# Strided half of x for two batches transposed by the DMA queue through the idle raw tile of k, with new lists for the order of the work

## The chip, the cores and the metric

The kernel runs on one core of one Trainium2 chip. The time is the device time of one execution, in microseconds (us). Before the change it is 287.94 us (median of three runs, 287.9 to 288.31). Other numbers come from one profiled execution of the same kernel, which took 288.18 us.

## The reference

Two layers in a row, on 8 batches of 576 tokens. Inputs are float32, and so is the output.

```python
# attention: q, k, v are (8, 8, 576, 64)
scores = q @ k^T / 8
mask_local   = (rel >= 0) & (rel < 32)                      # heads 0 to 3
mask_strided = (rel >= 0) & (pos_k % 32 == pos_q % 32)      # heads 4 to 7
attn = softmax(where(mask, scores, -1e9)) @ v
# mlp: x is (4608, 512), w_in (512, 2048), w_out (2048, 512)
x = attn.transpose(0, 2, 1, 3).reshape(4608, 512)
h = x @ w_in
out = (h * tanh(softplus(h))) @ w_out
```

## The kernel before, in words

The 4608 tokens of the second layer are worked in nine blocks of 512 (`t` = 0 to 8); the attention works in eight batches of 576 (`b` = 0 to 7). While block `t` goes through the second layer, batch `t + 1` goes through the attention, so that block `t + 1` finds its x. The x of the last four batches lies transposed in one ring, `xT`: 128 partitions by four chunks of columns. Chunks 0 and 1 hold the local heads, chunks 2 and 3 the strided ones.

**The second layer.** Each of its two matrix products is written as seven products of half size instead of eight (sums of weights and of x are made on VectorE). A block's first product goes in four groups `g`. In a list, `5:2` is product 5 of group 2, four matmuls of 256 columns; `1c`, `5c` are copies out of PSUM, `6c` and `7c` additions on VectorE that product 7 and product 4 wait for; `E`, `H`, `Z` are the activations on ScalarE; `x:0` to `x:3` are the sums of x. The second product of block `t - 1` runs in block `t`: `m5:0` is half of product 5, eight matmuls; `m1c`, `m5c`, `m6c`, `m7c`, `m3c`, `m4c` empty its banks, `g:1` to `g:3` and `n` are sums of the activations (`gs`), `st` stores the result.

**The attention.** `ld` loads a raw tile by GpSimd's queue (`ks`, `qs`: the strided heads; `kl`, `ql`: the local ones; `vs`, `vl`: the values). Batches 0 to 2 are transposed by TensorE (`T`, with the copy `t`), later ones by DMA transposes that SyncE (SP) issues (`D`). `q:s0` makes scores, `e` the exponentials, `k` multiplies by the mask, `v` is the product with the values, and `r` divides by the sums into `x_s` (72 partitions, strided) or `x_l` (96, local). `sp` and `sh` spread and share the values. From batch 2 on, `x_l` goes into `xT` by two DMA transposes of SP (`y:0`, `y:1`), and `x_s` by TensorE: `X:0:a` is eight transposes (line 322) into the spare PSUM bank `at`, and `xc:0:a:D` the copy from there into `xT` (line 112 on VectorE). `hold` is a small copy on GpSimd that waits for the DMA transposes of x, so that the loads queued behind it are issued after them.

**Order.** Nothing is reordered by a scheduler: the lists (`IN`, `SECOND`, `THIRD`, `MAIN`, `PLAIN`, `LAST`) are played word by word, and each engine works off its own instructions in that order, waiting on semaphores where an operand or a buffer isn't free. `IN` is the start and block 0, `SECOND` block 1, `THIRD` block 2, `MAIN` blocks 3 to 6 (batches 4 to 7), `PLAIN` blocks 7 and 8, which have no attention beside them, and `LAST` the second product of block 8. The loads of batch `b` are issued in blocks `b - 2` and `b - 3`; after batch 7 there are none left.

## Time and profile before

| | |
|---|---|
| median of the runs | 287.94 us |
| profiled execution | 288.18 us |
| its span, first to last instruction | 286.4 us |
| TensorE busy (matmuls) | 277.1 us, 97% |
| VectorE busy | 222.3 us, 78% |
| ScalarE busy | 193.8 us, 68% |
| GpSimd busy | 53.6 us, 19% |
| granted TensorE clock | 1.000 |

Blocks start, by TensorE's timeline, at about 59 us (block 1), 77 (block 2), 106.1, 134.7, 163.2 and 191.8 (blocks 3 to 6), 220.3 and 245.4 (blocks 7 and 8); block 8's second product begins at 270.

How to read it: a matmul's duration in the rows is from its issue to its modelled end, and matmuls overlap in the array, so what one costs in a dense stretch is the step from its start to the start of the next. In a row of the timeline stand the start, the duration of the group, engine, line, operation, tiles (written <- read), forms and the count; in brackets the idle time before it and what ended that. "SPq" and "POOLq" rows are issues of DMAs. Tiles `set`, `ee` and `at` are PSUM banks.

### The profile page before, as it was taken

The numbers are of one execution on the slowest core, as the hardware profiler recorded it, in microseconds if no ns is written. First come the engines' busy times: TensorE is split into PE (matmuls) and PEld (weight loads), VectorE is DVE, ScalarE is ACT, GpSimd is POOL, SyncE is SP. The second block draws the span as 40 slices with busy tenths as digits, with TensorE's granted clock in tenths as the row PEclk, the third lists the DMA queues.
The fourth block names the chain that finished last, engine by engine and source line by source line (L and its number), as shares of the span: only waits on it lengthen the run. The fifth ranks groups of instructions, "written<-read, shape, count | busy, mean of one in ns | idle before, by whom it ended". The sixth has DMA issues, their size and how long they took to land.

```text
span 286.4 us, 7693 instructions
## 1 busy us (share of the span) xinstructions
PE 277.1 (97%) x3274; PEld 227.8 (80%) x3274; DVE 222.3 (78%) x378; ACT 193.8 (68%) x293; POOL 53.6 (19%) x66
## 2 busy tenths in 40 slices
PE   8789999989999999999999999999999999999994
PEld 3556845658988898988899889988898888888884
DVE  1388869799998897989698969896989666756652
ACT  3686883499769777669776977697769127506920
POOL 8424241250007001700350054001000000000000
PEclk9999999999999999999999999999999999999999
DMA  6999999999959989999899979997050021003003
GB/s 102 176 206 201 205 183 199 110 219 163 150 95 92 127 145 113 233 153 155 228 141 131 179 199 165 127 176 203 11 190 2 2 94 54 0 3 146 2 0 146
DMA packets 101394, 37.45 MB, mean 131 GB/s; under 512 B 83040, under 2 KB 96992, under 8 KB 101360
## 3 DMA queue, kind: packets, MB, share of 16 engines
q0 software_dynamic: 61824, 18.85, 65.3%
q1 hardware_dynamic: 39248, 17.86, 26.7%
q8 instruction: 25, 0.41, 0.6%
q10 hardware_dynamic: 288, 0.25, 0.3%
q14 instruction: 9, 0.07, 0.1%
HBM read 37.87 MB, written 9.44 MB: 165 GB/s over the span
## 4 chain that ended last, share of the span: by engine, by line
PE 91%; DMA 3%; DVE 2%; ACT 1%; issue 1%; POOL 1%; DVEq 0%; ACTq 0%; POOLq 0%
PE set L121 57%; PE ee L121 21%; PE at L291 5%; PE at L121 4%; DMA vraw<-in_v_dram 3%; PE at L322 1%; PE ee L192 1%; PE ee L322 1%; DVE ee L115 0%; DVE qTl L112 0%; PE set L291 0%; PE ee L186 0%; ACT gT L649 0%; DVE x_l L305 0%; POOL ks L126 0%
## 5 line engine op out<-in xcount | busy, mean ns | idle before, releaser
L121 PEld LDWEIGHTS <-wis 128*128 128x128 bf16 x578 | 55.9, 98 | 11.4 <-issue 2.6
L121 PEld LDWEIGHTS <-gs 128*128 128x128 bf16 x512 | 48.8, 98 | 6.0
L121 PEld LDWEIGHTS <-gT 128*128 128x128 bf16 x448 | 42.1, 98 | 9.5
L121 PEld LDWEIGHTS <-w_in 128*128 128x128 bf16 x436 | 40.9, 97 | 8.6 <-issue 1.3
L121 PE MATMUL set<-w_out,gT 128*128 128x256 bf16 (+1 forms) x304 | 46.8, 295 | 0.0
L121 PE MATMUL set<-xT,w_in 128*128 128x256 bf16 (+1 forms) x296 | 45.7, 278 | 0.5 <-ACT set L110 0.3
L121 PE MATMUL set<-xs,wis 128*128 128x256 bf16 x280 | 42.0, 272 | 0.2 <-DVE ee L115 0.2
L420 ACT ACTIVATE gT<-set 128x1024 bf16<-128x1024 f32 x35 | 35.9, 1025 | 8.0 <-PE set L121 7.9
L110 ACT COPY set<-set 128x512 f32<-128x512 f32 x36 | 20.7, 574 | 18.4 <-PE set L121 17.9
L115 DVE TENSOR_TENSOR hh<-set,hh 128x512 f32<-128x512 f32 x35 | 24.0, 686 | 7.2 <-PE set L121 6.2
L115 DVE TENSOR_TENSOR ee<-set,hh 128x512 f32<-128x512 f32 x35 | 24.4, 697 | 5.7 <-PE set L121 5.3
L121 PE MATMUL set<-wos,gs 128*128 128x256 bf16 x224 | 28.5, 273 | 0.0
L416 ACT ACTIVATE gT<-ee 128x512 bf16<-128x512 f32 x35 | 20.2, 597 | 3.4 <-PE ee L121 3.2
L418 ACT ACTIVATE gT<-hh 128x512 bf16<-128x512 f32 x35 | 21.6, 632 | 0.9 <-DVE hh L115 0.6
L638 POOL COPY hold<-xT 1x2 bf16<-1x2 bf16 x6 | 3.3, 556 | 100.5 <-DMA xT<-x_l 98.5
L115 DVE TENSOR_TENSOR gs<-gT,gs 128x2048 bf16<-128x2048 bf16 x16 | 19.5, 1217 | 2.0 <-PE at L121 1.8
L121 PE MATMUL ee<-xs,wis 128*128 128x256 bf16 x140 | 21.0, 273 | 0.0
L121 PE MATMUL set<-xs,w_in 128*128 128x256 bf16 x140 | 21.0, 272 | 0.0
L121 PE MATMUL ee<-xT,wis 128*128 128x256 bf16 x140 | 21.0, 273 | 0.0
L115 DVE TENSOR_TENSOR gs<-gT 128x2048 bf16<-128x2048 bf16 x16 | 19.4, 1215 | 0.0
L305 DVE TENSOR_TENSOR x_s<-at,rden 72x768 bf16<-72x768 f32 (+1 forms) x22 | 18.8, 856 | 0.8
L266 DVE TENSOR_TENSOR Pl<-Pl,consts_sb 128x768 bf16<-128x768 bf16 x21 | 11.6, 554 | 8.6 <-ACT Pl L258 6.4
(127 smaller groups left out, 450.9 us busy)
## 6 DMA issues: line engine op xcount, KB each, us to landing
...
ks<-in_k_dram POOLq DMA_DIRECT2D x8, 288.0 KB, 10.6
qs<-in_q_dram POOLq DMA_DIRECT2D x8, 288.0 KB, 10.0
vraw<-in_v_dram POOLq DMA_DIRECT2D x8, 288.0 KB, 8.9
ql<-in_q_dram POOLq DMA_DIRECT2D x8, 288.0 KB, 10.3
vl<-in_v_dram POOLq DMA_DIRECT2D x8, 288.0 KB, 12.0
...
```

The costliest lines, as they stand in the source:

```text
L110: Sc.copy(out_, in_)
L115: eng.tensor_tensor(out=out_, in0=a, in1=b, op=op)
L121: PE.matmul(o, lhsT=lhsT, rhs=rhs, start=start, stop=stop, skip_group_check=True)
L192: PE.transpose(tr[64 * e:64 * e + 64, PL * j:PL * j + PL], src[0:PL, 2 * hp + e, j, :], ident[0:PL, 0:PL],)
L266: meng.tensor_tensor(out=pm, in0=pm, in1=mk[0:n, :].unsqueeze(1).unsqueeze(1).to_broadcast([n, 2, nu, w]), op=ALU.mult,)
L291: PE.matmul(po[:, (n - n0) // per, (n - n0) % per, :], lhsT=pt[0:r, c0:c0 + 128], rhs=rhs, start=True, stop=True,)
L305: Dv.tensor_tensor(out=xo, in0=po[0:m, :, :, 0:D], in1=rd.unsqueeze(3).to_broadcast([m, nb, per, D]), op=ALU.mult,)
L322: PE.transpose(tr[:, n * j:n * j + n], x[0:n, u:u + 2, :].rearrange("p u d -> p (u d)"), ident[0:n, 0:n],)
L416: Sc.activation(o[:, 0:2, 256:512], two(E), AF.Mish)
L418: Sc.activation(o[:, 2:4, 256:512], two(h[:, 1, :]), AF.Mish)
L420: Sc.activation(o[:, :, 0:256].rearrange("p (b u) n -> p b u n", b=2), SET[z][:, 0:2, :].rearrange("p b (u n) -> p b u n", u=2), AF.Mish,)
L638: Po.tensor_copy(hold[0:1, 0:2], src)
```

## The change

In blocks 5 and 6 the strided x of batches 6 and 7 no longer goes through TensorE. `V` is one DMA transpose issued by SP: it reads `x_s` (80 rows, of which the last eight are zeros now written once at the start) and writes sixteen transposed pieces into `ks`, the raw tile of k, which no load needs again at that point. `vc:0` and `vc:1` then copy them, with a stride, into chunks 2 and 3 of `xT`. `V` stands at the end of block 5 and of block 6; the copies stand early in the following block, both on VectorE in block 6, one on ScalarE and one on VectorE in block 7. Blocks 5, 6 and 7 get lists of their own (`M5`, `M6`, `P7`), and all other lists are written anew with the same words in another order, and with some copies on another engine. In the diff most of the lists' rows are left out.

```diff
@@ -312,6 +312,19 @@
             nc.sync.dma_start_transpose(
                 xT[:, c, t0:t0 + S].rearrange("p (u n) -> p u n", u=NW),
                 x_l[0:WQ, 12 * c:12 * c + 12, :].rearrange("p u d -> p (u d)"),
+            )
+
+        def xs_dma(self):
+            nc.sync.dma_start_transpose(
+                flat(ks)[:, 0:16 * SU].rearrange("c (u n) -> c u n", u=16),
+                x_s[0:SU].rearrange("p u d -> p (u d)"),
+            )
+
+        def xs_copy(self, hf, eng):
+            t0 = (self.b % RING) * S
+            cast(
+                eng, xT[:, 2 + hf, t0:t0 + S].rearrange("p (n j) -> p n j", j=CS),
+                flat(ks)[:, 8 * SU * hf:8 * SU * hf + 8 * SU].rearrange("p (j n) -> p n j", j=CS)[:, 0:PN, :],
             )
 
         def xt(self, kind, hf, bank):
@@ -529,6 +542,7 @@
         Sc.dma_start(consts[:], consts_h.ap())
         for x in (ks, qs):
             nc.sync.dma_start(x[PN:SU].rearrange("p h x -> p (h x)"), zeros_h.ap())
+        nc.sync.dma_start(x_s[PN:SU].rearrange("p u d -> p (u d)"), zeros_h.ap())
         Dv.memset(wis[:, 0:2, 0, 0, :], 0.0)
 
         at = {}
@@ -629,6 +643,10 @@
                 at[b].xt_copy("sl"[f == "yc"], int(x[0]), BANK[x[1]], eng)
             elif f == "y":
                 at[b].xt_dma(int(x[0]))
+            elif f == "V":
+                at[b].xs_dma()
+            elif f == "vc":
+                at[b].xs_copy(int(x[0]), eng)
             elif f == "D":
                 for n in x:
                     transpose_by_dma(n)
@@ -682,80 +700,106 @@
...
         IN = (
-            "ae un:1:a un:1:a un:1:a ld:ks@0 un:1:a un:1:a un:1:a un:1:a un:1:a ld:qs@0 clear:0 ld:kl@0 b:s1:C@0 "
...
+            "ld:ks@0 ld:qs@0 un:1:a un:1:a un:1:a un:1:a un:1:a un:1:a un:1:a un:1:a clear:1 clear:0 b:s1:C@0 "
+            "un:1:a un:1:a un:1:a un:1:a T:ks0:e@0 un:1:a T:ks1:f@0 ld:kl@0 t:ks0:e:A@0 b:s0:B@0 ae t:ks1:f:D@0 "
+            "T:qs0:e@0 T:qs1:f@0 t:qs0:e:D@0 un:1:a b:s2:A@0 un:1:e ld:vs@0 sp:D un:1:e t:qs1:f:A@0 q:s2:A:b@0 "
+            "un:1:e e:s2:A@0 q:s1:C:b@0 q:s0:B:b@0 e:s1:C@0 e:s0:B@0 ld:ql@0 T:kl1:f@0 t:kl1:f:A@0 un:1:e "
...
         SECOND = (
-            "so:1:D so:2:D T:ql1:f x:0 q:s0:A so:3:D t:ql1:f:D x:1 sh:D e:s0:A T:ql0:e q:s1:H ld:ks@3 t:ql0:e:D "
-            "1:0 e:s1:H 1c:0:D q:s2:A e:s2:A k:s2:D q:l0:H x:3 5:0 q:l1:A e:l0:H q:l2:H sp:D 2:0 5c:0:A k:s0:D "
-            "6:0 x:2 e:l2:H 1:1 e:l1:A 1c:1:A 5:1 6c:0 7:0 k:l1:D 5c:1:A 2:1 6:1 ld:vl@3 v:s0:A k:s1:D 3:0 7c:0 "
...
+            "x:0 T:ql1:f so:1:D so:2:D so:3:D t:ql1:f:D x:1 q:s0:A e:s0:A T:ql0:e t:ql0:e:D q:s1:H 1:0 q:s2:A "
+            "e:s1:H sp:D sh:D q:l0:H 1c:0:D e:s2:A 5:0 e:l0:H q:l1:A q:l2:H x:2 k:s1:D x:3 5c:0:A 2:0 e:l2:H 6:0 "
+            "ld:ks@3 k:s2:D 6c:0 k:s0:D e:l1:A 1:1 5:1 7:0 7c:0 1c:1:A 2:1 5c:1:A 6:1 6c:1 v:s0:A r:s0:A 3:0 4:0 "
...
         MAIN = (
+            "m1c:A g:1 ae g:2 m5:0 m2:0 x:0 q:l0:A e:l0:A q:l1:F m2:1 m6:0 e:l1:F q:s0:F e:s0:F sh:D q:l2:A "
+            "k:l0:D m6:1 e:l2:A m6c:D k:l1:D x:1 m5:1 x:2 q:s2:F q:s1:A e:s2:F e:s1:A m7:0 m7:1 m5c:A D:ks@{n1} "
...
+        M5 = (
+            "x:0 m5:0 ld:kl@{n2} m1c:A m5:1 m2:0 q:l0:A g:1 q:l1:F g:2 m2:1 ae sh:A e:l1:F e:l0:A m6:0 k:l1:D "
+            "q:s0:F m5c:D e:s0:F k:l0:D q:l2:A m6:1 m6c:D m3:0 ld:qs@{n2} e:l2:A k:s0:D x:2 q:s2:F e:s2:F q:s1:A "
+            "k:s2:D g:3 D:ks@{n1} e:s1:A m7:0 m7:1 m7c x:1 m3:1 v:l0:A k:s1:D ld:ql@{n2} am 1:0 1c:0:A m4:0 m4:1 "
+            "5:0 ld:ks@{n2} m3c 2:0 ld:vl@{n1} k:l2:D 6:0 r:l0:A sp:D m4c:A 1:1 5c:0:A x:3 D:kl@{n1} 1c:1:A 6c:0 "
+            "5:1 v:l1:A 7:0 2:1 6:1 5c:1:D 7c:0 4:0 Z:0 H:0 D:ql@{n1} 6c:1 3:0 7:1 r:l1:A 3:1 1:2 7c:1 E:0 v:s0:A "
+            "4:1 5:2 1c:2:A 2:2 6:2 E:1 r:s0:A 5c:2:D 6c:2 v:s1:A r:s1:A Z:1 1:3 1c:3:A 5:3 7:2 7c:2 2:3 6:3 "
+            "5c:3:A 6c:3 H:1 v:s2:A D:qs@{n1} H:2 r:s2:A n 4:2 Z:2 V 3:2 E:2 y:1 y:0 7:3 7c:3 hold 3:3 E:3 H:3 "
+            "st:1 ^m1:0 ld:vs@{n1} ^m1:1 4:3 Z:3 st:0 "
+        )
+        M6 = (
+            "m5:0 m5:1 ae m1c:D m5c:A g:1 m2:0 m2:1 q:l1:F e:l1:F q:l0:A k:l1:D e:l0:A m6:0 g:2 m6:1 q:l2:A g:3 "
+            "q:s0:F m3:0 m6c:A m7:0 e:s0:F vc:1:D@6 q:s2:F k:s0:D e:l2:A q:s1:A e:s2:F vc:0:D@6 x:0 m7:1 m7c "
+            "k:l2:D x:1 1:0 e:s1:A 5:0 1c:0:A k:l0:D m3:1 x:2 m3c 2:0 x:3 5c:0:A 6:0 6c:0 k:s1:D am m4:0 m4:1 "
+            "sh:A v:l0:A m4c:A 3:0 E:0 r:l0:A 7:0 7c:0 st:0 1:1 5:1 sp:D 1c:1:A v:l1:A 2:1 5c:1:A r:l1:A 6:1 6c:1 "
+            "4:0 5:2 5c:2:D y:0 v:s0:A 7:1 Z:0 st:1 7c:1 1:2 H:0 1c:2:A 3:1 4:1 Z:1 E:1 2:2 6:2 r:s0:A v:s1:A "
+            "k:s2:D 1:3 1c:3:A H:1 6c:2 r:s1:A 5:3 7:2 7c:2 5c:3:A 2:3 6:3 y:1 v:s2:A 4:2 hold 6c:3 3:2 7:3 H:2 "
+            "r:s2:A 3:3 Z:2 E:2 ^m1:0 7c:3 n 4:3 E:3 ^m1:1 V H:3 Z:3 "
+        )
+        P7 = (
+            "m5:0 1:0 m1c:A 1c:0:A vc:1:A@7 m2:0 m2:1 g:1 g:2 m6:0 m6:1 vc:0:D@7 x:2 m6c:A x:0 m5:1 m7:0 g:3 x:1 "
+            "m5c:A m7:1 m7c 5:0 x:3 m3:0 5c:0:D m4:0 m4:1 m4c:A m3:1 2:0 6:0 1:1 m3c 5:1 1c:1:A 5c:1:A 6c:0 7:0 "
+            "7c:0 2:1 6:1 4:0 Z:0 6c:1 st:0 3:0 7:1 7c:1 3:1 1:2 E:0 1c:2:D 4:1 H:0 5:2 Z:1 2:2 6:2 E:1 1:3 5:3 "
+            "1c:3:A st:1 5c:2:D 6c:2 5c:3:A 7:2 7c:2 H:1 2:3 6:3 4:2 Z:2 3:2 E:2 6c:3 7:3 7c:3 H:2 H:3 3:3 E:3 "
+            "^m1:0 ^m1:1 4:3 n Z:3 "
         )
         PLAIN = (
-            "m5:0 g:1 x:0 x:1 m1c:A m2:0 m2:1 5:0 m6:0 m6:1 m5:1 g:2 m5c:D g:3 m6c:A m7:0 m7:1 m7c x:2 1:0 5c:0:D "
-            "m3:0 m4:0 m4:1 m4c:A m3:1 1c:0:D 2:0 6:0 m3c 1:1 1c:1:A 6c:0 x:3 5:1 7:0 7c:0 5c:1:A 2:1 6:1 6c:1 "
-            "4:0 Z:0 3:0 E:0 7:1 3:1 1:2 7c:1 4:1 E:1 Z:1 5:2 1c:2:D 2:2 6:2 H:0 5c:2:D 6c:2 1:3 1c:3:A 5:3 7:2 "
-            "7c:2 5c:3:A H:1 H:2 2:3 6:3 6c:3 4:2 st:0 3:2 Z:2 7:3 3:3 E:2 ^m1:0 7c:3 n E:3 H:3 st:1 4:3 Z:3 "
-            "^m1:1 "
+            "x:0 x:1 5:0 m5:0 m1c:D m2:0 m2:1 g:1 x:3 5c:0:D m6:0 m6:1 m5:1 g:2 m6c:A m7:0 g:3 m7:1 m5c:A m3:0 "
+            "1:0 1c:0:A m7c m4:0 x:2 m4:1 m3:1 2:0 6:0 m4c:A 1:1 1c:1:A m3c 5:1 5c:1:A 6c:0 7:0 7c:0 2:1 6:1 4:0 "
+            "3:0 6c:1 7:1 3:1 Z:0 1:2 st:0 E:0 1c:2:A 5:2 E:1 7c:1 4:1 5c:2:D Z:1 2:2 6:2 5:3 H:0 1:3 1c:3:A 6c:2 "
+            "7:2 7c:2 H:2 3:2 2:3 6:3 5c:3:D 6c:3 H:1 ^m1:0 n 4:2 7:3 ^m1:1 E:2 Z:2 7c:3 H:3 3:3 st:1 E:3 4:3 Z:3 "
         )
...
         for t in range(3, NBLK):
+            main = {5: M5, 6: M6}.get(t, MAIN)
             if t + 1 < B:
-                go(" ".join(w for w in MAIN.format(n1=t + 2, n2=t + 3).split() if int(w.partition("@")[2] or 0) < B), t)
+                go(" ".join(w for w in main.format(n1=t + 2, n2=t + 3).split() if int(w.partition("@")[2] or 0) < B), t)
             else:
-                go(PLAIN, t)
+                go(P7 if t + 1 == B else PLAIN, t)
         go(LAST, NBLK)
```

On SP, around the end of block 5 (`kTs`, `kTl`, `qTl`, `qTs` are the transposed tiles of batch 7, `osb` a block's result), before:

```order
L172 DMA_TRANSPOSE kTs<-ks 128x16x80
L172 DMA_TRANSPOSE kTl<-kl 128x12x128
L172 DMA_TRANSPOSE qTl<-ql 128x12x96
L172 DMA_TRANSPOSE qTs<-qs 128x16x80
L312 DMA_TRANSPOSE xT<-x_l 128x6x96 x2
L525 DMA out_dram<-osb 128x2x512 x2
L312 DMA_TRANSPOSE xT<-x_l 128x6x96 x2
L525 DMA out_dram<-osb 128x2x512 x6
```

and now:

```order
L172 DMA_TRANSPOSE kTs<-ks 128x16x80
L172 DMA_TRANSPOSE kTl<-kl 128x12x128
L172 DMA_TRANSPOSE qTl<-ql 128x12x96
L172 DMA_TRANSPOSE qTs<-qs 128x16x80
L318 DMA_TRANSPOSE ks<-x_s 128x16x80
L312 DMA_TRANSPOSE xT<-x_l 128x6x96 x2
L538 DMA out_dram<-osb 128x2x512 x3
L312 DMA_TRANSPOSE xT<-x_l 128x6x96
L538 DMA out_dram<-osb 128x2x512
L312 DMA_TRANSPOSE xT<-x_l 128x6x96
L318 DMA_TRANSPOSE ks<-x_s 128x16x80
L538 DMA out_dram<-osb 128x2x512 x4
```

The transpose of `x_s` stands between that of batch 7's q and those of batch 6's `x_l`; in block 6 it is the last one.

On VectorE, at the start of block 6 (`gs` and `xs` are sums, `Pl` and `Ps` the exponentials being masked, `o` and `osb` results of the second product), now:

```order
L115 TENSOR_TENSOR gs<-gT,gs 128x2048
L266 TENSOR_TENSOR Pl_88<-Pl_88,consts_sb 128x2x384
L115 TENSOR_TENSOR gs<-gT 128x2048
L115 TENSOR_TENSOR gs<-gT,gs 128x2048
L112 COPY xT<-ks 128x576
L266 TENSOR_TENSOR Ps_84<-Ps_84,consts_sb 72x2x432
L112 COPY xT<-ks 128x576
L115 TENSOR_TENSOR xs<-xT 128x512
L115 TENSOR_TENSOR osb<-set_101,o_66 128x2x256
```

The two copies from `ks` stand behind three sums and a mask, and ahead of the first sum of x (`x:0`); before, the copies into `xT` stood at the end of the block before.

On VectorE, where block 1 begins (`wos` are sums of w_out, `kTs` and `qTl` copies of batch 2's transposes, `vl` is `sh`, `vs` is `sp`), before:

```order
L112 COPY kTs<-ee_104 128x8x72
L112 COPY kTs<-ee_103 128x8x72
L115 TENSOR_TENSOR wos<-w_out 128x2048
L115 TENSOR_TENSOR wos<-wos,w_out 128x2048
L115 TENSOR_TENSOR xs<-xT 128x512
L115 TENSOR_TENSOR wos<-w_out,wos 128x2048
L112 COPY qTl<-ee_104 128x576
L115 TENSOR_TENSOR xs<-xT,xs 128x512
L112 COPY vl_78<-vl_78 32x4x5x64
L112 COPY qTl<-ee_103 128x576
L112 COPY set_101<-set_101 128x512
```

and now:

```order
L112 COPY kTs<-ee_104 128x8x72
L115 TENSOR_TENSOR xs<-xT 128x512
L115 TENSOR_TENSOR wos<-w_out 128x2048
L115 TENSOR_TENSOR wos<-wos,w_out 128x2048
L115 TENSOR_TENSOR wos<-w_out,wos 128x2048
L112 COPY qTl<-ee_104 128x576
L115 TENSOR_TENSOR xs<-xT,xs 128x512
L112 COPY qTl<-ee_103 128x576
L112 COPY vs<-vraw 72x32x64
L112 COPY vl_78<-vl_78 32x4x5x64
L112 COPY set_101<-set_101 128x512
```

One of the two copies into `kTs` has gone to ScalarE, and the second copy into `qTl` now stands ahead of the copies of the values.

More of the change, by code (lines that the diff above doesn't have):

```diff
@@ L684 @@
         IN = (
[23 rows of a table removed]
[23 rows of a table added]
         )
         SECOND = (
[7 rows of a table removed]
[7 rows of a table added]
         )
         THIRD = (
[10 rows of a table removed]
[10 rows of a table added]
         )
         MAIN = (
[8 rows of a table removed]
[8 rows of a table added]
+        )
+        M5 = (
[8 rows of a table added]
+        )
+        M6 = (
[7 rows of a table added]
+        )
+        P7 = (
[5 rows of a table added]
         )
         PLAIN = (
[5 rows of a table removed]
[4 rows of a table added]
         )
         LAST = (
-            "g:1 m5:0 m5:1 m1c:A m6:0 g:2 m6:1 m2:0 m6c:A m7:0 m7:1 g:3 m5c:A m7c m2:1 m3:0 m3:1 z:b:D m4:0 m3c "
-            "m4:1 w:b:S z:1:A z:0:D w:1:A st:1 w:0:S "
+            "m1c:D g:1 m5:0 m5:1 m5c:A g:2 m6:0 m6:1 g:3 m2:0 m6c:A m2:1 m7:0 m7:1 m7c z:b:D w:b:S m3:0 m3:1 m3c "
+            "st:1 m4:0 m4:1 z:1:A z:0:D w:0:S w:1:A "
         )
```

83 rows, old and new, of tables (IN, MAIN, SECOND, THIRD) are left out of this document.

## The prediction

> **What bounds the kernel now.** I read the shares of the page first, then the chain of waits, then busy time by block.
>
> ```profile
> span 286.4 us, 7693 instructions
> ...
> PE 277.1 (97%) x3274; PEld 227.8 (80%) x3274; DVE 222.3 (78%) x378; ACT 193.8 (68%) x293; POOL 53.6 (19%) x66
> ...
> PE 91%; DMA 3%; DVE 2%; ACT 1%; issue 1%; POOL 1%; DVEq 0%; ACTq 0%; POOLq 0%
> ```
>
> TensorE is 91% of the chain that ended last. Where its idle time lies, busy time in stretches shows (columns: stretch, its length, then busy us and instructions of each engine):
>
> ```profile
> 0.00:13.30 13.30, 10.50 (x112) 5.22 (x113) 2.91 (x18) 6.99 (x9) 8.88 (x16) 1.00 1.01 136
> ...
> 59.70:77.60 17.90, 16.85 (x212) 14.29 (x206) 17.25 (x30) 15.40 (x27) 2.23 (x3) 1.00 1.43 181
> ...
> 191.80:220.30 28.50, 28.50 (x354) 24.92 (x353) 24.58 (x41) 22.13 (x34) 1.08 (x3) 1.00 0.39 111
> 220.30:245.40 25.10, 25.10 (x233) 21.89 (x231) 16.71 (x25) 12.50 (x20) 0.00 (x0) 1.00 0.11 43
> 245.40:270.10 24.70, 24.70 (x223) 21.44 (x221) 15.83 (x23) 12.03 (x19) 0.00 (x0) 1.00 0.12 44
> ```
>
> In blocks 5 to 8 TensorE has no idle time, at a granted clock of 1.00. Work taken from it there comes off the end one to one, as long as VectorE, busy 24.58 of 28.50 us in block 6, keeps up. Real waits are left at the start, which is bound by loads (the 16 DMA engines 1.01 busy), and around block 1.
>
> **The transposes removed.** Four groups of eight (line 322) go, two for batch 6 and two for batch 7. TensorE's timeline in block 6:
>
> ```profile
> 192.25 0.42 PE L322 MATMUL at<-consts_sb,x_s 72*128 72x72 bf16 x8
> 192.51 1.04 PE L121 MATMUL set<-w_out,gT 128*128 128x256 bf16 x8
> ...
> 217.50 0.42 PE L322 MATMUL at<-consts_sb,x_s 72*128 72x72 bf16 x8
> 217.75 0.60 PE L121 MATMUL set<-xs,w_in 128*128 128x256 bf16 x4
> ```
>
> From the start of a group to the start of what follows is 0.25 to 0.26 us, some 32 ns a transpose. 4 x 0.26 = **1.04 us**. Bounds: nothing, if VectorE becomes the limit there, and 1.04. The Trainium skill (TensorE: Matmul & The Clock Gate, Back-to-back issue gap) gives pairs of weight load and matmul about 81 ns apiece at 128 columns; by that the 32 would be worth about 2.6 us, an estimate from the page. The trace's 32 ns decides against it, and it enters no sum.
>
> **The copies in their place.** The copies out of `at` are VectorE's today, 745 to 758 ns each. Nothing in the trace is a strided copy out of an SBUF tile of this shape; the nearest rows are a 128x512 sum in SBUF and the strided copy out of PSUM:
>
> ```profile
> L115 DVE TENSOR_TENSOR xs<-xT x18: 410/418/425, 21.8 to 255.4; 128x512 bf16<-128x512 bf16 x18
> L112 DVE COPY xT<-at x12: 745/754/758, 72.3 to 221.3; 128x576 bf16<-128x576 bf16 x12
> L110 ACT COPY xT<-ee x5: 633/638/645, 21.0 to 51.4; 128x576 bf16<-128x576 bf16 x5
> ```
>
> So 0.42 to 0.75 us on VectorE; I take 0.65, since the read has the same stride. Three copies there instead of four, and one of some 0.64 on ScalarE: no more work than before, but moved from the end of a block, where TensorE doesn't wait for it, to its first third, ahead of `x:0`, which product 5 of group 0 needs.
>
> **Does V land in time?** The DMA rows (median us from issue to landing) and SP's and GpSimd's timelines:
>
> ```profile
> kTs<-ks SPq DMA_TRANSPOSE x5, 3.9
> qTs<-qs SPq DMA_TRANSPOSE x5, 4.3
> ```
> ```profile
> 183.71 1.59 SPq L172 DMA_TRANSPOSE kTs<-ks  x1
> 185.40 1.86 SPq L172 DMA_TRANSPOSE kTl<-kl  x1
> 187.34 1.60 SPq L172 DMA_TRANSPOSE qTl<-ql  x1
> 189.04 1.63 SPq L172 DMA_TRANSPOSE qTs<-qs  x1
> 190.78 3.27 SPq L312 DMA_TRANSPOSE xT<-x_l  x2
> ```
>
> V has the shape of `kTs<-ks`: 1.6 us of SP and about 4 to landing. Batch 7: after the last norm that V waits for, TensorE still has 3:3, m1:0, 4:3, m1:1, m5:0, 1:0, m2 and m6, seventeen steps of four matmuls at 0.43 to 0.44 us (rows 259.34 and 259.77 below), so 7.4 us, before `m6c` must run on ScalarE; V and `vc:1`, queued ahead of it there, take 3.9 + 0.64 = 4.5. Hidden, with 2.9 us to spare; without that cover up to 4.5 would be lost. Batch 6: SP reaches V behind `qTs` about where it reached `x_l` before, 190.8, lands at 195, and `vc` stands behind sums and a mask at about 199. Hidden too. V's cost on the path: **0**.
>
> What V is put ahead of is late instead: the two transposes of `x_l` move back by V's 1.6 us, then the `hold` on GpSimd, then the load of batch 7's values behind it:
>
> ```profile
> 195.29 0.18 POOL L638 COPY hold<-xT 1x2 bf16<-1x2 bf16 x1 [20.58 <-DMA xT<-x_l]
> 195.88 0.73 POOL L141 DMA_DIRECT2D vraw<-in_v_dram  x1 [0.41 <-issue]
> ```
> ```profile
> vraw<-in_v_dram POOLq DMA_DIRECT2D x8, 288.0 KB, 8.9
> ```
> ```profile
> 206.39 0.68 DVE L112 COPY vs<-vraw 72x2048 bf16<-72x2048 bf16 x1
> ```
>
> They land at 195.88 + 8.9 = 204.8 and are copied at 206.39: 1.6 us to spare, which V's 1.6 uses up. The new list puts `sp` behind a sum, a mask and a second sum that came after it (`6c:0`, `k:s1`, `7c:0`), some 1.4 us later by my count. Just hidden, cost **0**, and the weakest point.
>
> **Block 1.** TensorE waits for VectorE's copies of batch 2's local q:
>
> ```profile
> 59.45 0.19 PE L121 MATMUL ee<-qTs,kTs 64*128 64x72 bf16 x1 [0.33 <-DVE qTl L112]
> ...
> 61.47 0.21 PE L121 MATMUL set<-qTl,kTl 64*128 64x96 bf16 x1 [0.89 <-DVE qTl L112]
> ```
> ```profile
> 54.05 0.82 DVE L112 COPY kTs<-ee 128x576 bf16<-128x576 bf16 x2 [0.60 <-PE ee L186]
> ...
> 58.65 0.75 DVE L112 COPY qTl<-ee 128x576 bf16<-128x576 bf16 x1
> ...
> 59.76 0.99 DVE L112 COPY vl<-vl 32x1280 bf16<-32x1280 bf16 x1
> 60.68 0.73 DVE L112 COPY qTl<-ee 128x576 bf16<-128x576 bf16 x1
> ...
> 64.23 0.70 DVE L115 TENSOR_TENSOR ee<-set,hh 128x512 f32<-128x512 f32 x1
> 64.84 0.56 DVE L266 TENSOR_TENSOR Pl<-Pl,consts_sb 128x768 bf16<-128x768 bf16 x1
> ```
>
> VectorE works without a gap from 54.05 to 64.9. One `kTs` copy goes to ScalarE (-0.37: two in 0.82, one in 0.45), and `sh` (0.92 from start to start) no longer stands ahead of the second `qTl`. The 0.33 wait shrinks to about nothing, the 0.89 one to some 0.3, where ScalarE's exponentials free the banks next. But the copies moved behind come before the sum at 64.23 that product 7 waits for, so only VectorE's shorter queue counts: **-0.35**. Bounds: 0, if that sum is held by a mask instead, and -0.9, if both waits were gained.
>
> **The orders of blocks 7 and 8.** In the plain blocks small steps are left where product 7 or 4 stands only two steps behind the sum's product:
>
> ```profile
> 259.34 0.60 PE L121 MATMUL set<-xT,w_in 128*128 128x256 bf16 x4
> 259.77 0.60 PE L121 MATMUL ee<-xs,wis 128*128 128x256 bf16 x4
> 260.29 0.60 PE L121 MATMUL set<-xs,wis 128*128 128x256 bf16 x4
> ```
>
> 0.52 us where 0.43 is clean. The old list has seven such places, the new one four (7:0, 4:0, 7:1, 7:2; elsewhere three steps or more stand between), so block 8 gives **-0.25**; block 7's list has seven still. Counted the same way, blocks 3 and 4 lose one place each: **-0.15**.
>
> **Start.** GpSimd's order is the same up to the second load of w_out, and the fillers (`un`) are eighteen before and now. The only thing added is 32 KB of zeros for `x_s`, 0.24 us at the 136 GB/s of the first stretch if the first values wait for it: **+0.1**, between 0 and 0.24. The rest of `IN` I take at 0, between -0.6 and +0.6: I find the same waits in the new order.
>
> **Blocks 5 and 6.** There VectorE has the least slack, and new neighbours: in block 5 `r:l1` ahead of `7c:1`, in block 6 `g:2` and `g:3` behind a mask and ahead of `vc`. Following the queues with the rows' steps, I find two or three waits of 0.1 us; with full durations in a row (0.70 for a sum whose step, 64.23 to 64.84, is 0.61) it would be 1.1. **+0.3**, between 0 and 1.1.
>
> The sum: -1.04 - 0.35 - 0.25 - 0.15 + 0.1 + 0.3 = -1.4 us. The span becomes 285.0 and the profiled execution, 1.8 us above its span as now, 288.18 - 1.4 = 286.8; the median lay 0.24 below the profiled one, so **286.5 us**.
>
> **Rivals.** (1) VectorE takes the gain back: both attention blocks run at its pace, and block 1's shorter queue ends at a mask. For it: 24.58 of 28.50 busy, and its copies now ahead of `x:0`; against it: no copy is added. Then +1.1 instead of +0.3 and 0 instead of -0.35: -0.25, 287.7. (2) The values of batch 7 come late: V and the `x_l` transposes take 2.8 us each of SP (as 72.98 below) instead of 1.6 and the load 12 (as vl's median) instead of 8.9.
>
> ```profile
> 72.98 2.78 SPq L172 DMA_TRANSPOSE kTl<-kl  x1
> ...
> 206.54 4.36 SPq L312 DMA_TRANSPOSE xT<-x_l  x2
> ```
> ```profile
> vl<-in_v_dram POOLq DMA_DIRECT2D x8, 288.0 KB, 12.0
> ```
>
> That is 2.8 + 2.3 of further transposes and 3.1 of load against 3.0 of room (1.6 + 1.4): 5.2 late at worst, about 3 in the middle, and everything behind `sp` in VectorE's order waits, TensorE with it. -1.4 + 3 = 289.5, slower. It decides from the point where the load lands later than `sp`'s turn, about 207.8. (3) The new orders are worth more than I can count: both waits of block 1 (-0.9) and 0.6 in `IN`: -1.4 - 0.55 - 0.6 = -2.55, 285.4.
>
> **How the numbers follow.** Forecast 0.60, rival 1 0.19, rival 2 0.10, rival 3 0.11. The forecast's own range is 285.8 to 287.2; to leave out no more than 2 in 10 it reaches over rivals 1 and 3, **285.1 to 288.1**. This kernel's runs tell about 0.2% (0.58 us) from no change: faster is under 287.4, so the forecast nearly whole and rival 3: 0.71. Same 0.19, slower 0.10.
>
> **What would show it.** Right: 64 transposes of `x_s` into `at` instead of 96, blocks 5 and 6 shorter by 0.5 us or a little less at 100% TensorE; `vc` in block 6 not waiting for a DMA; the wait of 0.89 in block 1 under 0.4. Wrong: an idle VectorE ahead of `vs<-vraw` or `xT<-ks` with a DMA as releaser, TensorE with gaps released by VectorE in blocks 5 and 6, or a start that differs by more than 0.6 us at block 1.

## The result, and the profile after

The changed kernel takes 287.09 us (median of 16 runs, 286.03 to 290.68); the kernel before, run beside it, 288.83 us (16 runs). The ratio is 0.9944, with a 95% interval of 0.9916 to 0.9972: faster by 0.56%, some 1.6 us. In a second series on another occasion it was 287.60 against 288.88, ratio 0.9943 (0.9908 to 0.9979). The profiled execution took 286.27 us instead of 288.18. Part of the difference of the medians is the granted clock: its mean is under 0.996 in 46 of 97 runs of the kernel before and in 5 of 28 of the change, and over the other runs the medians are 288.17 and 287.05, 1.1 us apart.

The page of the change, as that of before was shown:

```profile
span 284.5 us, 7631 instructions
...
PE 275.3 (97%) x3242; PEld 226.5 (80%) x3242; DVE 219.5 (77%) x375; ACT 193.6 (68%) x296; POOL 53.8 (19%) x66
...
PE 89%; DMA 3%; ACT 3%; DVE 2%; issue 1%; POOL 1%; ACTq 0%; DVEq 0%; POOLq 0%
```

The shares are the same within two points; TensorE has 32 matmuls fewer. To see where the time went, I cut both traces at the same places: a block ends with the last matmul of its first product and of `m1`, block 0 with its second product. Busy time in these stretches, of the kernel before (blocks 1, 5, 6 and 8):

```profile
57.70:78.02 20.32, 18.95 (x258) 15.92 (x257) 19.64 (x33) 17.82 (x30) 3.55 (x4) 1.00 1.44 178
...
164.81:193.38 28.57, 28.57 (x354) 25.00 (x352) 24.66 (x41) 22.21 (x34) 6.60 (x7) 1.00 1.29 167
193.38:221.95 28.57, 28.57 (x354) 24.99 (x352) 24.65 (x41) 22.20 (x34) 1.08 (x3) 1.00 0.35 102
...
247.02:272.16 25.14, 25.14 (x227) 21.84 (x225) 16.27 (x24) 12.47 (x20) 0.00 (x0) 1.00 0.11 43
```

and of the change (blocks 1, 3, 5, 6 and 8):

```profile
57.37:77.12 19.75, 19.18 (x257) 16.05 (x257) 17.82 (x31) 18.17 (x32) 3.56 (x4) 1.00 1.49 172
...
106.53:135.15 28.62, 28.62 (x355) 25.00 (x353) 24.87 (x42) 21.36 (x34) 6.78 (x7) 1.00 1.23 161
...
163.76:191.79 28.03, 28.03 (x339) 24.55 (x337) 24.05 (x41) 20.68 (x32) 6.54 (x7) 1.00 1.36 165
191.79:219.98 28.19, 28.19 (x339) 24.58 (x337) 23.90 (x40) 23.37 (x35) 2.20 (x3) 1.00 0.67 142
...
245.04:269.90 24.86, 24.86 (x227) 21.88 (x224) 15.49 (x22) 12.76 (x20) 0.00 (x0) 1.00 0.11 43
```

Read the length behind the colon pair: block 1 from 20.32 to 19.75, block 5 from 28.57 to 28.03, block 6 from 28.57 to 28.19, block 8 from 25.14 to 24.86. All stretches together, in us:

```
                        before   change   difference
start, to 13.35          13.34    13.36      +0.02
block 0                  44.36    44.01      -0.35
block 1                  20.32    19.75      -0.57
blocks 2 to 4            86.79    86.64      -0.15
block 5                  28.57    28.03      -0.54
block 6                  28.57    28.19      -0.38
block 7                  25.07    25.06      -0.01
block 8                  25.14    24.86      -0.28
last product             10.47    10.51      +0.04
after the last matmul     3.78     4.06      +0.28
span                    286.41   284.47      -1.94
```

(Blocks 2 to 4 are taken together, since eight transposes moved from the start of block 3 to the end of block 2.) The 0.28 at the end comes with V, whatever the lists: the stretch after the last matmul takes 4.01 to 4.09 us in all nine traces of kernels with V, those of the experiments below included, and 3.70 to 3.78 in all five without. The trace shows SP there in nine waits for semaphores, one behind the other, which the timeline leaves out. The wait that ends with the last store, 2.9 us after the start of the last matmul in both, was the eighth of them before. In the change it is the third, and six more of some 0.06 us apiece come behind it. Why V changes their order was not tried.

What became of the strided x, by the tile's rows, SyncE's and VectorE's timelines and the row of ScalarE:

```profile
L335 PE MATMUL at<-consts_sb,x_s x64: 193/197/198, 70.9 to 162.9; 72*128 72x72 bf16 x64
```
```profile
192.34 1.90 SPq L318 DMA_TRANSPOSE ks<-x_s  x1
194.33 3.82 SPq L312 DMA_TRANSPOSE xT<-x_l  x2
...
217.62 1.32 SPq L318 DMA_TRANSPOSE ks<-x_s  x1
```
```profile
199.40 0.71 DVE L112 COPY xT<-ks 128x576 bf16<-128x576 bf16 x1
...
200.55 0.71 DVE L112 COPY xT<-ks 128x576 bf16<-128x576 bf16 x1
```
```profile
222.02 1.31 ACT L110 COPY xT<-ks 128x576 bf16<-128x576 bf16 x1
```

64 transposes instead of 96. V takes SP 1.90 and 1.32 us. The second lands after 3.4 us; for the first the trace has no landing time. No copy waits for either. The copy costs 0.71 us on VectorE and 1.31 on ScalarE.

### The profile page after: what moved, and what is told of

The parts are those of the page before. It is cut to its first block, busy times and chain, and to the rows that moved or that the text cites. A ratio compares the mean times of both kernels' runs of the same rounds, so it can differ in the third digit from the quotient of the medians.

```text
span 284.5 us, 7631 instructions
## 1 busy us (share of the span) xinstructions
PE 275.3 (97%) x3242; PEld 226.5 (80%) x3242; DVE 219.5 (77%) x375; ACT 193.6 (68%) x296; POOL 53.8 (19%) x66
## 4 chain that ended last, share of the span: by engine, by line
PE 89%; DMA 3%; ACT 3%; DVE 2%; issue 1%; POOL 1%; ACTq 0%; DVEq 0%; POOLq 0%
PE set L121 57%; PE ee L121 21%; PE at L291 4%; PE at L121 4%; DMA vraw<-in_v_dram 3%; PE at L335 1%; PE ee L335 1%; ACT osb L110 1%; DVE x_s L305 0%; ACT kTl L110 0%; ACT gT L667 0%; ACT Ps L258 0%; DVE x_l L305 0%; ACT qTs L110 0%; ACT Ps L260 0%
## 5 line engine op out<-in xcount | busy, mean ns | idle before, releaser
L121 PEld LDWEIGHTS <-wis 128*128 128x128 bf16 x578 | 55.7, 98 | 11.2 <-issue 2.4
L121 PE MATMUL set<-w_out,gT 128*128 128x256 bf16 (+1 forms) x304 | 46.2, 295 | 0.0
L110 ACT COPY set<-set 128x512 f32<-128x512 f32 x37 | 21.4, 577 | 18.8 <-PE set L121 18.3
L121 PE MATMUL set<-wos,gs 128*128 128x256 bf16 x224 | 27.8, 273 | 0.0
L121 PE MATMUL ee<-wos,gT 128*128 128x256 bf16 x128 | 16.1, 273 | 0.0
```

What stands on the lines that cost most here:

```text
L110: Sc.copy(out_, in_)
L121: PE.matmul(o, lhsT=lhsT, rhs=rhs, start=start, stop=stop, skip_group_check=True)
```

## The experiments

All times are medians, with the ratio to the kernel before in the same series. "Old lists" are those of before.

**Lists and transposes apart.** The first pair takes the change in two halves: its lists with the transposes back on TensorE, and V in the old lists.

```diff
 M5
-... r:s2:A n 4:2 Z:2 V 3:2 E:2 y:1 y:0 7:3 7c:3 hold 3:3 ... 4:3 Z:3 st:0
+... r:s2:A n 4:2 Z:2 X:0:a 3:2 E:2 y:1 y:0 xc:0:a:D 7:3 7c:3 hold 3:3 ... 4:3 X:1:A Z:3 st:0 xc:1:A:D
 M6: the same at its end, and no vc:1:D@6, vc:0:D@6
 P7: no vc:1:A@7, vc:0:D@7
```

> The change's lists without its transposes: batches 6 and 7 go through TensorE again, eight transposes and a copy from the bank at the end of blocks 5 and 6, twice each, as before the change; V and vc are gone. Theory (the 32 transposes are worth 32 ns each on TensorE and the rest of the gain is the lists'): blocks 5 and 6 become 0.45 to 0.55 us longer each than in the change (28.02 to about 28.5 and 28.19 to about 28.7), all other blocks stay, so 1.0 us slower than the change and still 0.6 us faster than before. Rival (the gain of blocks 5 and 6 is their new lists', and VectorE's pace hides what TensorE saves): no longer than the change by more than 0.2 us.

289.68 us, ratio 1.0019 (0.9998 to 1.0040): much slower than either theory said, in the main because of where I had put `X:0`. TensorE's timeline in block 5:

```profile
190.10 0.60 PE L121 MATMUL set<-xs,w_in 128*128 128x256 bf16 x4
191.68 0.42 PE L335 MATMUL at<-consts_sb,x_s 72*128 72x72 bf16 x8 [0.97 <-DVE x_s L305]
```

The norm on VectorE had not written `x_s` yet. V at this place in the list cost no wait: SP came to it only at 192.34, behind four other transposes, and `x_s` had been ready since 189.4. In block 6 SP does wait for the norm there, and TensorE goes on meanwhile. So one thing V gives is freedom of place, apart from the matmuls it saves. To price the transposes I moved them two to three products later.

```diff
 M5
-... X:0:a 3:2 E:2 y:1 y:0 xc:0:a:D 7:3 7c:3 hold ...
+... 3:2 E:2 y:1 y:0 7:3 X:0:a 7c:3 xc:0:a:D hold ...
 M6
-... r:s2:A X:0:a 3:3 Z:2 E:2 xc:0:a:D ^m1:0 7c:3 ...
+... r:s2:A 3:3 Z:2 E:2 ^m1:0 X:0:a 7c:3 xc:0:a:D ...
```

> The same as the run with the change's lists alone, but with TensorE's transposes two to three products later in blocks 5 and 6 and their copies behind the additions of product 7 (7c), so that TensorE doesn't stand waiting for the norm of x_s (0.97 us of block 5 there, at 191.68). Theory (32 ns a transpose): block 5 at 28.55 and block 6 at 28.7, 0.5 each above the change. Rival (the transposes cost TensorE more than their own time in these orders, by their place in its queue): still 0.8 us or more above the change in one of the two blocks, with a wait of TensorE at X.

Busy time of blocks 5 and 6:

```profile
165.33:193.88 28.55, 28.44 (x346) 24.79 (x344) 24.54 (x41) 20.78 (x32) 6.15 (x7) 1.00 1.43 165
193.88:222.57 28.69, 28.69 (x355) 25.18 (x353) 22.95 (x39) 23.37 (x35) 1.08 (x3) 1.00 0.44 109
```

and TensorE's timeline around the first and the last eight of the transposes:

```profile
190.30 0.60 PE L121 MATMUL set<-xs,wis 128*128 128x256 bf16 x4
191.01 0.42 PE L335 MATMUL at<-consts_sb,x_s 72*128 72x72 bf16 x8
191.26 0.60 PE L121 MATMUL ee<-xT,wis 128*128 128x256 bf16 x4
...
222.57 0.42 PE L335 MATMUL at<-consts_sb,x_s 72*128 72x72 bf16 x8
223.40 0.83 PE L121 MATMUL ee<-wos,gs 128*128 128x256 bf16 x6 [0.41 <-DVE gs L115]
```

In the change's other traces these two blocks took 28.03 and 28.19. Block 6 is the clean price: 16 more transposes (355 matmuls instead of 339), no idle time, 0.50 us longer, so 31 ns each. Block 5 is 0.52 us longer, the figure that the theory had, but by coincidence: as cut here it holds only eight transposes, at 191.01, 0.25 us by their step. The other 0.27 are a wait for the norm again, since the four matmuls before them need 0.44 us and 0.71 went by. The last eight, at 222.57, fall into block 7. Four groups at 0.25 to 0.26 from start to start are 1.03 us for the 32.

The whole kernel took 289.02 us, ratio 0.9995 (0.9971 to 1.0020). That is some 1.5 us above the change. The transposes are 1.03 of it, and two waits that this edit made are 0.85: the 0.27, and 0.58 at the start of block 7 by the steps, for a sum of the activations queued behind a copy `xc`. The end, without V, gives 0.35 back. **The lists without V, with the transposes at these places, gain nothing that can be measured**; without the two waits they would stand some 0.8 us under the kernel before, an estimate from these rows.

The other half, with the copies early in blocks 6 and 7:

```diff
+main = MAIN
+if t > 4:
+    for w in ("X:0:a ", "V "), ("xc:0:a:D ", ""), ("X:1:A xc:1:A:D ", ""):
+        main = main.replace(*w)
+if t == 6:
+    main = main.replace("g:2 e:l2:A ", "g:2 e:l2:A vc:1:D@6 vc:0:D@6 x:0 ").replace("g:1 x:0 ", "g:1 ")
...
+if t == 7:
+    plain = plain.replace("g:1 x:0 x:1 m1c:A m2:0 ", "g:1 m1c:A m2:0 vc:1:A@7 vc:0:D@7 ").replace(
+        "m2:1 5:0 m6:0 m6:1 m5:1 g:2 m5c:D ", "m2:1 m6:0 m6:1 m5:1 g:2 x:0 x:1 m5c:D 5:0 ")
```

> The transposes alone: the lists of before, and only X, xc of batches 6 and 7 replaced by V at the place of X:0 and vc early in the next block (both on VectorE in block 6, one on ScalarE in block 7); V stands behind the transposes of x_l here, so the values of batch 7 are not pushed back. Theory: blocks 5 and 6 shorter by 0.5 us each (28.57 to about 28.05), nothing else moves: 0.9 to 1.0 us faster than before. Rival 1 (VectorE takes it back, since its copies now stand ahead of x:0): blocks 6 and 7 lose 0.3 us or more by waits on VectorE, the sum is 0 to 0.4 us faster.

291.79 us, ratio 1.0073 (1.0042 to 1.0103): slower than before. Block 5 took 28.19 us, 0.38 less; block 6 took 29.39, 0.82 more. Its VectorE and TensorE:

```profile
200.46 1.34 DVE L112 COPY xT<-ks 128x576 bf16<-128x576 bf16 x2
201.84 0.43 DVE L115 TENSOR_TENSOR xs<-xT 128x512 bf16<-128x512 bf16 x1
202.18 0.55 DVE L266 TENSOR_TENSOR Pl<-Pl,consts_sb 128x768 bf16<-128x768 bf16 x1
202.65 0.68 DVE L112 COPY o<-set 128x512 f32<-128x512 f32 x1
```
```profile
203.38 0.81 PE L121 MATMUL set<-wos,gs 128*128 128x256 bf16 x6 [0.99 <-DVE o L112]
```

`m6c` (`o<-set`), for which TensorE's product 7 waits, stands behind both copies, a sum and a mask. I moved the copies and gave `m6c` to ScalarE:

```diff
-main.replace("g:2 e:l2:A ", "g:2 e:l2:A vc:1:D@6 vc:0:D@6 x:0 ").replace("g:1 x:0 ", "g:1 ")
+("g:1 x:0 ", "g:1 "), ("m6c:D ", "m6c:A "), ("m5c:D ", "m5c:D vc:1:D@6 "),
+("m7:0 g:3 x:1 5:0 m7:1 m3:0 ", "m7:0 vc:0:D@6 x:0 x:1 g:3 m7:1 m3:0 5:0 "),
```

> The transposes alone, with the lists of before, as in the first run of that kind, but in block 6 the first copy vc stands behind m5c, the second behind the mask k:s2, m6c runs on ScalarE, and x:0, x:1 and 5:0 come behind. There TensorE had waited 1.17 us at 202.19 for m6c, queued on VectorE behind both copies. Theory (that wait was the place of the copies alone): block 6 falls from 29.39 to about 28.2, block 5 stays at 28.2, so 0.7 to 0.8 us faster than before in all. Rival (VectorE is the limit in block 6 wherever the copies stand): block 6 stays above 28.6, and the sum is under 0.4 us faster.

290.61 us, ratio 1.0052 (1.0025 to 1.0079). Block 5 took 28.19 again, block 6 as much as 30.00: now three waits, the longest ahead of product 4, whose sum `m7c` stood behind the second copy, two sums of x and `g:3`. The rival's numbers came, but two tries at a place are no proof that the old order has none. What they show: **V alone, at these two places, loses**, since two copies of 0.7 us on VectorE early in an attention block meet work that TensorE waits for. From block 5 to the end these two profiles lose 0.8 and 1.4 us to that of the kernel before. What they lose ahead of block 5, 2.35 and 2.15 us, lies where the lists are the old ones and goes with stretches at half the clock (last section), so it is not put down to V. The change's list for block 6 has `m1c` on VectorE and both `m5c` and `m6c` on ScalarE, and there the same two copies cost next to nothing: block 6 is 0.38 us shorter than before, of the 0.52 that its 16 transposes took.

**Block 1.** First the change's whole list for block 1 in the old kernel (the string `SECOND`, nothing else).

> The lists of before, with the change's SECOND alone (block 1). Theory (the shorter queue on VectorE, sh behind the second qTl copy, is what block 1 gained): block 1 goes from 20.42 to about 20.0 us, 0.35 to 0.55 faster than before. Rival (the ks copy that IN moved to ScalarE, or what IN leaves ready, is the gain): block 1 shorter by less than 0.15 us.

289.13 us, ratio 1.0021 (0.9985 to 1.0058). Block 1 took 19.91 us, 0.41 less, and block 2 took 29.82, 0.57 more: the old list of block 2 begins with `sh` and `m1c` on VectorE, and the new list leaves VectorE two masks and a sum to do first. TensorE waited 0.35 and 0.25 us there. Gained and given back at the joint. Then one word alone:

```diff
 SECOND
-... T:ql1:f x:0 q:s0:A so:3:D t:ql1:f:D x:1 sh:D e:s0:A T:ql0:e q:s1:H ld:ks@3 t:ql0:e:D
+... T:ql1:f x:0 q:s0:A so:3:D t:ql1:f:D x:1 e:s0:A T:ql0:e q:s1:H ld:ks@3 t:ql0:e:D sh:D
```

> The lists of before, with one word of block 1 moved: sh, the sharing of batch 2's values on VectorE, from ahead of the second qTl copy to behind it. With the change's whole list for block 1 that block took 19.91 us instead of 20.31. Theory (the 0.92 us of sh ahead of qTl was what the scores of batch 2 waited for): the wait of 0.89 shrinks to 0.3 or less, and block 1 takes 20.0 to 20.15. Rival (the sum ahead of product 7 or a mask limits block 1 whatever stands first): the wait of 0.89 shrinks, but block 1 stays above 20.2, the gain given back before its end.

One profiled execution, without a ratio. Block 1 took 19.79 us, 0.53 less than before and all but 0.04 of the change's gain. What is left of the waits, in TensorE's timeline, and VectorE's rows there:

```profile
60.64 0.19 PE L121 MATMUL ee<-qTs,kTs 64*128 64x72 bf16 x1 [0.33 <-DVE qTl L112]
...
62.10 0.20 PE L121 MATMUL ee<-qTl,kTl 64*128 64x96 bf16 x1 [0.22 <-ACT Ps L258]
```
```profile
60.84 0.75 DVE L112 COPY qTl<-ee 128x576 bf16<-128x576 bf16 x1
61.61 0.48 DVE L112 COPY vl<-vl 32x1280 bf16<-32x1280 bf16 x1
```

The 0.89 is now 0.22 and ends with ScalarE's exponentials. `sh` itself takes 0.48 us at its new place; ahead of `qTl` it had taken 0.99. Those 0.51 us are the gain: the same copies, sums and masks stand ahead of the sum that product 7 waits for, and it starts 6.02 us into the block instead of 6.53.

**Room for the values of batch 7.** V issued twice, so that `hold` and the load come later still:

```diff
 M5
-... 4:2 Z:2 V 3:2 E:2 y:1 y:0 ...
+... 4:2 Z:2 V V 3:2 E:2 y:1 y:0 ...
```

> The change with V issued twice in block 5, the same transposes to the same place, ahead of the two transposes of x_l: SP gets 1.9 us more to issue (5 us if the second waits for the first to land), hold and the load of batch 7's values come as much later. Rival 2 of the prediction (the load has no room left): vs is copied 2 to 5 us later than 208.0 and waits for a DMA, TensorE loses 1 us or more in block 6. Against it (room is left, since the copy waited for nothing at 208.0): VectorE waits under 0.5 us and block 6 stays within 0.2 us of 28.19.

SP's, GpSimd's and VectorE's timelines, then the load's time from issue to landing, alone in its window:

```profile
193.09 5.45 SPq L318 DMA_TRANSPOSE ks<-x_s  x2
198.63 2.57 SPq L312 DMA_TRANSPOSE xT<-x_l  x2
```
```profile
203.19 0.73 POOL L141 DMA_DIRECT2D vraw<-in_v_dram  x1
```
```profile
209.96 0.68 DVE L112 COPY vs<-vraw 72x2048 bf16<-72x2048 bf16 x1
```
```profile
DMA to landing us min/median/max: 5.5/5.5/5.5
```

The copy at 209.96 waited for nothing, and block 6 took 28.19 again. The dose was smaller than meant: counted from the start of block 6, the load was issued 1.1 us later than in the change, not 2 to 5. It took 5.5 us there, and not the 8.9 of its row over the whole kernel, which mixes in the loads of other stages (11.2 and 8.8 us for batches 3 and 4 before). In the change itself:

```profile
199.47 0.69 POOL L656 COPY hold<-xT 1x2 bf16<-1x2 bf16 x1 [23.87 <-DMA xT<-x_l]
200.11 1.39 POOL L141 DMA_DIRECT2D vraw<-in_v_dram  x1
```
```profile
208.01 0.68 DVE L112 COPY vs<-vraw 72x2048 bf16<-72x2048 bf16 x1
```

The load took 6.1 us and was there at 206.2, 1.8 us ahead of its copy. In every trace with the change's lists of blocks 5 and 6, this run's included, it took 4.8 to 6.2 us and was there 1.2 us or more ahead: rival 2 did not come, at batch 7.

**Block 3.** But the same run lost 1.7 us elsewhere: its block 3 took 30.33 us. The copy of batch 4's values there had waited 2.37 us for the load. The traces of the two runs with the change's lists and the old transposes (29.26 and 30.30 us) had that too, and I ran the change again for a second profile.

> The change itself once more, on the same chip as the run above and with a second profile. If the late values of batch 4 belong to the change's lists, its block 3 takes 29.3 to 30.3 us in this profile as in the other three, and the first profile's 28.62 was the better case; if they came from the edits of those runs, it takes 28.6 again. In both cases blocks 5 and 6 take 28.0 and 28.2.

Block 3 took 29.51 us in it (blocks 5 and 6: 28.03 and 28.19). GpSimd's issue, VectorE's copy and the load's time:

```profile
111.95 0.70 POOL L141 DMA_DIRECT2D vraw<-in_v_dram  x1 [0.16 <-issue]
```
```profile
120.02 0.70 DVE L115 TENSOR_TENSOR ee<-set,hh 128x512 f32<-128x512 f32 x1
121.92 0.69 DVE L112 COPY vs<-vraw 72x2048 bf16<-72x2048 bf16 x1 [1.20 <-DMA vraw<-in_v_dram]
```
```profile
DMA to landing us min/median/max: 9.9/9.9/9.9
```

Over all traces: with the change's order around this load, five times, it took 8.7 to 10.9 us, and its copy waited 0.18 us once and 1.2 to 2.4 us the other times (block 3: 28.62 to 30.33). With the old order, five times, it took 8.4 to 10.1, and the copy waited 0.22 and 0.62 us in two and not at all in three. From its issue to its copy's turn there are 8.6 to 9.3 us in the change and 8.6 to 10.3 in the old order. I tried three ways to give it room, all in the list of block 2. First ahead of the load of batch 5's strided q, which waits on GpSimd for a transpose until 110.5:

```diff
 THIRD
-... D:qs 6c:1 ld:qs@5 H:0 7:1 3:1 sp:D E:0 v:s0:A@3 5:2 1c:2:A ld:vs@4 E:1 ...
+... D:qs 6c:1 ld:vs@4 ld:qs@5 H:0 7:1 3:1 sp:D E:0 v:s0:A@3 5:2 1c:2:A E:1 ...
```

> The change, with the load of batch 4's values issued ahead of the load of batch 5's strided q in block 2, and not behind it; that one waits for a DMA transpose until 110.5. In the traces so far the copy of these values in block 3 waited 0.18 us (the change), 0.22 (before), 1.29 and 2.37 (two runs of the change's lists), as the load took 8.7 to 10.9 us. Theory: issued at about 97 to 98 us, landed by 108, so that wait goes, block 3 is 28.4 to 28.6 in every run, and the median is 0.3 to 0.8 us under the change's. Rival (the load now runs against the transposes of batch 4's k and q, 99.9 to 107.5, and makes them late): block 3's first scores wait, and the gain is lost or turns to a loss of 0.3 us or more.

295.68 us, ratio 1.0221 (1.0184 to 1.0258). This was a mistake: it puts the load ahead of `sp` too, so `sp` waits for it and batch 3's attention is computed with batch 4's values, a wrong result. It serves as a large dose of late values:

```profile
108.29 0.69 DVE L112 COPY vs<-vraw 72x2048 bf16<-72x2048 bf16 x1 [8.40 <-DMA vraw<-in_v_dram]
```

Block 2 took 39.64 us, 10.2 more: TensorE stood idle for 8.06 us of the 8.40 that VectorE waited for values, and lost some 2 us more, most of it in a stretch at half the clock behind it (last section shows the like). The edit that was meant leaves the load where it is, behind `sp`, and moves the load of q behind it:

```diff
 THIRD
-... 6c:1 ld:qs@5 H:0 7:1 3:1 sp:D E:0 v:s0:A@3 5:2 1c:2:A ld:vs@4 E:1 ...
+... 6c:1 H:0 7:1 3:1 sp:D E:0 v:s0:A@3 5:2 1c:2:A ld:vs@4 ld:qs@5 E:1 ...
```

> The change, with the load of batch 5's strided q moved behind the load of batch 4's values on GpSimd's queue in block 2. So far the load of q stood ahead of it and waited until 110.5 for a DMA transpose; the values were issued at 111.4, and their copy in block 3 waited 0.18 us for them in the change's profile, but 1.3 to 2.4 in three other traces with the same lists, where the load took 10.6 to 10.9 us and not 8.7. Theory: the values are issued at 97 to 98 us, landed by 110, that wait is gone and block 3 takes 28.4 to 28.6 us; the median comes 0.3 to 1.0 us under that of the change in the same call. Rival (the load now runs beside the transposes of batch 4's k and q, 99.9 to 107.5, and makes them late): block 3's first scores wait, and it is no faster, or slower by 0.3 us or more.

287.25 us, ratio 0.9923 (0.9888 to 0.9958); the change in the same series 0.9943 (0.9908 to 0.9979), so no difference that can be told. Both mechanisms came: the values were issued at 97.42 and never waited for, and the transposes ran late, by TensorE's timeline:

```profile
111.74 0.19 PE L121 MATMUL set<-qTs,kTs 64*128 64x72 bf16 x1 [0.64 <-DMA qTs<-qs]
```

Block 3 took 29.93 us. Then `hold` first, as it had stood before the change:

```diff
 THIRD
-... y:1@3 ld:ql@5 y:0@3 1:3 ... ld:kl@5 Z:2 H:2 X:0:a@3 ^m1:0 hold@3 7c:3 ...
+... y:1@3 y:0@3 hold@3 ld:ql@5 1:3 ... ld:kl@5 Z:2 H:2 X:0:a@3 ^m1:0 7c:3 ...
```

> The change, with hold of batch 3 moved ahead of the loads of batch 5's local q and k on GpSimd's queue, as it stood before the change. In the change these two loads are issued right behind the values of batch 4 (112.2 and 113.4 us) and beside the two transposes of x_l; before, GpSimd waited in hold until 114.7 first, and the values had the queue to themselves. Theory (that is why the values of batch 4 took 9.9 to 10.9 us in four traces with the change's lists, and 8.4 to 10.1 with the old ones, and why the sum x:1 and product 4 in block 3 waited for x_l): the load takes 8.4 to 9.4 us, block 3 takes 28.4 to 28.7 us and not 29.5, blocks 5 and 6 stay, and the median is 0.4 to 0.9 us under the change's 287.1 to 287.6. Rival (the time of this load scatters by itself): block 3 takes 29.0 or more, or the median stays within 0.3 us of the change's.

287.73 us, ratio 0.9962 (0.9928 to 0.9996). The load took 10.5 us all the same and block 3 took 29.84: my theory fell, the loads issued behind it are not what makes it long. Last, 3 us sooner, behind a `hold` on batch 4's `kTs`:

```diff
 THIRD (on top of the one above)
-... 6c:1 ld:qs@5 H:0 ... 1c:2:A ld:vs@4 E:1 ...
+... 6c:1 H:0 ... 1c:2:A hold:ks ld:vs@4 ld:qs@5 E:1 ...
```

> As the run above, and the values of batch 4 are issued ahead of the strided q of batch 5, behind a hold that waits only until batch 4's strided k has been transposed (about 108 us, 3 us sooner). Issued at 97 without such a hold they had made the transposes late, and TensorE had waited 0.81 us for qTs. Theory (2 to 3 us more room for the load, and only the last transposes beside it): the copy of the values doesn't wait at all, block 3 takes 28.4 to 28.6, the median is as in the run above or up to 0.3 us lower. Rival (the load still runs against the transposes of qTs and x_l): TensorE waits 0.3 us or more for qTs or for a sum of x, and block 3 is longer than in the run above.

289.62 us, ratio 1.0017 (0.9978 to 1.0056). The load took 5.9 us now, but the transposes of `x_l` beside it came so late that a sum of x waited:

```profile
116.79 0.42 DVE L115 TENSOR_TENSOR xs<-xT,xs 128x512 bf16<-128x512 bf16 x1 [3.09 <-DMA xT<-x_l]
```

Block 3 took 32.88 us. Values, strided q and the transposes of x are all under way in the same 10 us; each order that was tried made another of them late. Why the load takes 8.7 us in one execution and 10.9 in the next stays open. None of these beats the change beyond the measurement.

## Why the prediction was right, and where not

The forecast held: 286.5 us, 1.4 less than before, against 287.09, and 1.74 less by the medians, 1.91 by the profiled executions. Faster had been given 0.71. The largest term, the transposes, and the hidden V came as reasoned. That the total came so near is partly luck: block 0 gave 0.35 that no term had, block 1 gave 0.57 for another reason than the one priced, V cost 0.28 at the end that no term had, and the late values of block 3 take back 0.6 to 1.7 in most profiles. By its terms, in the order of the sum:

- **Transposes, -1.04.** -1.03 by their steps, and 0.50 for 16 of them in the run that puts them back. The rule of the Trainium skill that had been weighed there, 81 ns a pair at 128 columns (TensorE: Matmul & The Clock Gate, Back-to-back issue gap), is no price for these 72 columns: they step at 32 ns.
- **Copies, 0.65 on VectorE and 0.64 on ScalarE, hidden.** 0.71 and 1.31. ScalarE's price was off by a factor of two, taken from a copy out of PSUM; block 7 hid it all the same (25.06 against 25.07), though VectorE waited 0.90 us for that copy. In block 6 it is the list that hides VectorE's copies; I had called them "no more work than before", and with the old list's order round them block 6 took 1.2 and 1.8 us more than in the change.
- **V hidden, 0.** Yes, in both blocks. At the end of the kernel it costs 0.28 all the same: the sum had no term for what follows the last matmul.
- **Values of batch 7, 0, "the weakest point".** 0, with 1.8 us to spare and not nil, as two errors partly cancel. One is the load's 8.9 us, the median over the kernel; the row of its own stretch in the kernel before has 5.9:

```profile
DMA to landing us min/median/max: 5.9/5.9/5.9
```

  The other is `hold`: it came 4.2 us later than before (199.47 against 195.29), not 1.6: SP's three transposes are issued 192.34 to 198.15 instead of 190.78 to 194.05. The mechanism of rival 2, values that come late, was at work, but for batch 4 in block 3. There the copy waits for its load even in the profile before, 0.22 us; batch 7's load had been there 4.6 us ahead. How busy the DMA engines are does not explain it alone: the share is 1.23 in block 3 and 1.40 in block 4 of the change, and block 4's load of values took 6.1 us. I had looked at the batch whose queue the change touches and not at the load with the least room.
- **Block 1, -0.35.** -0.57, and not for the reason given. The step that failed is "only VectorE's shorter queue counts: -0.35": that priced the `kTs` copy moved to ScalarE, which adds next to nothing (19.79 without it, 19.75 with it), and put the move of `sh` at nothing. I charged `sh` at its new place in full, but it takes 0.48 us there and not 0.99, so the sum that product 7 waits for comes earlier as well; that move alone gave 0.53.
- **Block 8, -0.25; block 7, 0; blocks 3 and 4, -0.15.** -0.28, -0.01, and -0.15 for blocks 2 to 4. Counting steps between a sum's product and its user came out for blocks 7 and 8. For blocks 3 and 4 the total is luck: with the eight moved transposes (0.26) set off, block 2 gave 0.10, block 3 gave 0.10 in the profile with the least wait for its values, and block 4 lost 0.05.
- **Start, +0.1.** +0.02. The zeros cost nothing that shows.
- **Rest of IN, 0.** -0.35 in block 0. I had found the same waits in both orders; one of some 0.17 us by the steps (ahead of the matmul at 47.27 before) is gone, and the rest I cannot name.
- **Order in blocks 5 and 6, +0.3.** The two blocks went from 57.14 to 56.22; with the 1.03 of the transposes added back that is +0.11.

The span gained 0.5 us more than the sum: -0.22 from block 1, -0.35 from block 0, -0.2 from blocks 5 and 6, -0.08 at the start, -0.03 in block 8, and +0.3 from the last product and the end. The median gained less than the profiled execution; 0.6 to 1.7 us go to the late values of block 3 in four of five profiles with the change's order there, which is a likely reason and not a shown one, since each profile is one execution.

**Rivals.** The first (VectorE takes it back) is what happens with V in the old lists, and doesn't in the change's. The third named block 1 and `IN`, rightly, and put them too high together. What no rival had: the two halves, as they were built here, do not add up. The lists alone measure 0.9995, V alone 1.0052 and 1.0073, both together 0.9944. Some 0.85 us of that are the waits that the first half's own edit made, and V alone was tried at two places only.
